# Attention with a compressive memory beside a gated FFN: VectorE's normalization put ahead of an eviction, a product with ones a chain sooner, three operations elsewhere in another order

## The chip, the cores and the metric

The kernel runs on one core of one Trainium2 chip. The metric is device microseconds of one launch. A core has a matrix engine (PE; its weight loads are listed apart as PEld), a vector engine (DVE), an activation engine (ACT), a general engine (POOL) and a queue that issues DMAs (SP). Each works through its own instructions in their order and waits for the others on semaphores.

## The reference, cut to what matters

Two branches read the same x (2048 x 576), and a gate mixes them.

```
for s in range(4):                     # 4 segments of 512, 32 heads of 18
    p = softmax(qs @ ks.T * scale + mask)
    a_dot = p @ vs
    o = g * (phi(qs) @ M) / (phi(qs) @ z) + (1 - g) * a_dot
    M, z = M + phi(ks).T @ vs, z + sum(phi(ks))
a = concat(o) @ wo
b = (gelu(x @ w_gate) * (x @ w_up)) @ w_down      # 576 -> 4608 -> 576
out = sigmoid(x . gate_w) * a + (1 - that) * b
```

## The kernel before, in words

Every large product is made of 16-bit words: a value is split into a high and a low word, and three products (high by high, high by low, low by high) stand for one. Ahead of the split each weight tile is scaled, by a factor from a sum of squares over the whole tile. The FFN products are further made by sums of sub-blocks, with fewer products and more additions.

Projections come first (to about 211 us), then one loop of 72 steps v (`step`, line 1427), then an output stage. PE, ACT, DVE and POOL take their instructions exactly in the order in which the code issues them, so the order written in `step` is the order on each engine. Steps go by fours: `fb = v // 4` is a block of two hidden tiles of the FFN, 18 in all, and `i4 = v % 4` is the place in it. Each step makes gate and up products for two of four column groups of x (into the PSUM banks V, X = tag G, Y = tag U), `gelu` (ACT), the product of the two halves `hidden` (DVE, line 1279, reads the banks G and U), their high and low words (ACT line 1286, POOL line 1294), and eight chains `down` of the block before: six matmuls into one of two buffers of the bank `dn` (line 1256) and an eviction into `acc` on DVE (line 1264, for block 0 line 1262).

Between those lie the attention's pieces. With `k = v - 4`, step v makes the scores of heads 2k and 2k + 1 (line 1171, banks st, dn, pv), adds mask and takes the row maximum on DVE (`piece`, line 1174), makes powers (`powers`: ACT lines 1190 and 1191, POOL line 1192, two transposing DMAs), and multiplies by the values two steps later (`values`, line 1209, bank pv). `normalize(k - 2)` (lines 1219 to 1226) is five DVE instructions which read that bank, divide by the row sums and add into `ob`; after them the bank pv is free.

At `i4 == 1` of every block but the first, `scales(fb + 1, ...)` makes the scale factors for the next block. Its `sums` (line 94) is the product of a matrix of ones with ten sums of squares (`stat`), in f32, which adds over the partitions. ACT has written those sums: `act_squares` at the start of the step, line 89, four activations and four reads of the accumulator. The product goes into the bank pv while the attention runs (fb 1 to 16), so it must wait for the normalization that empties it. Six small DVE instructions follow (lines 268 to 275, on 128 x 2 or 128 x 4 elements). `scales_out` on POOL (lines 281 to 289) ends the work later in the step.

Other places that matter here: `scale_d` (line 394) scales two tiles of the next down weights, in place, on DVE; POOL's `sums_g` (lines 330 to 335) adds weight blocks; `nest_pairs_x` (ACT line 481, DVE line 483) splits sums of x; `result_low` (line 1239) makes the low words of a finished group of four heads, which go to DRAM and are read back, transposed, for the output stage.

The order around the change, at `i4 == 1` (the copy at line 1524 evicts the bank U; X has the tag G, Y has U):

```
product(Y, f, S2, t, 4, 6)
g0 = gl_tile(); dve.tensor_copy(g0, Y)          # L1524
if on(k - 2) and on(k): normalize(k - 2)        # L1219-1226
product(X, f, A12, x1, 2, 6)
rest(X, f, U4, x1, (0,))                        # L1302 into G
some(fb - 1, early[2:3])                        # one chain down
scales(fb + 1, bank("pv") if on(k) else None)   # L94, L268-275
product(Y, f, S1, t, 0, 2)                      # L532 into U
```

Of the kernel before, what the change touches and what calls it, by code (L numbers as in the profile page):

```python
# [26 lines left out]
NF = F // P  # L27
NB = NF // 2
# [15 lines left out]
def kernel(ctx: ExitStack, tc: tile.TileContext, xs, wqk, wv, wo, wgu, wd, beta, out):  # L44
# [8 lines left out]
    def bank(tag, bufs=1, dt=F32):  # L53
        return ps.tile([P, 512 if dt == F32 else 1024], dt, name=tag, tag=tag, bufs=bufs)
# [36 lines left out]
    def sums(st, o=None):  # L91

        o = (spare() if o is None else o)[:, : st.shape[1]]
        pe.matmul(o, ones, st, start=True, stop=True)  # L94
        return o
# [168 lines left out]
    def scales(fb, o=None):  # L264

        o = sums(stat[fb % 2].rearrange("p a b -> p (a b)"), o)
        z = wts.tile([P, 6], F32, name="z", tag="z", bufs=2)
        dve.tensor_reduce(z[:, 4:6], o.rearrange("p (a b) -> p a b", a=2), AX.X, OP.add)  # L268
        dve.tensor_scalar(z[:, 0:4], x2, z[:, 4:5], 1e-30, OP.mult, OP.max)
        v = wts.tile([P, 2, 2], F32, name="v", tag="v", bufs=2)  # L270
        pb = wts.tile([P, 2, 4], F32, name="pb", tag="pb", bufs=3)
        dve.tensor_scalar(v[:, 0].bitcast(I32), z[:, 4:6].bitcast(I32), 1, EXP, OP.logical_shift_right, OP.bitwise_and)
        dve.tensor_scalar(pb[:, 0].bitcast(I32), z[:, 0:4].bitcast(I32), EXP, None, OP.bitwise_and)
        dve.tensor_scalar(v[:, 1].bitcast(I32), v[:, 0].bitcast(I32), EXP, None, OP.bitwise_xor)
        dve.tensor_scalar(pb[:, 1].bitcast(I32), pb[:, 0].bitcast(I32), EXP, None, OP.bitwise_xor)
        scl_a[fb] = v, pb
# [27 lines left out]
    def scale_g(f, cols=slice(0, KT * P)):  # L304
        if f < NF:
            r = raw_g[f].rearrange("p (a b) -> p a b", a=2)[:, :, cols]
            dve.tensor_scalar(r, r, scl[f // 2][0][:, 0:1], None, OP.mult)
# [16 lines left out]
    def sums_g(f):  # L324
        if f >= NF:
            return
        r = raw_g[f]
        g0, g2, u0, u2 = (r[:, o : o + 2 * P] for o in (0, 2 * P, KW, KW + 2 * P))
        g4, u4 = r[:, 4 * P : KW], r[:, KW + 4 * P :]
        pool.tensor_tensor(g2, g0, g2, OP.add)  # L330
        if f < 2 or f % 2 == 0:
            pool.tensor_tensor(g0, u0, g0, OP.subtract)
        pool.tensor_tensor(u0, g2, u0, OP.subtract)
        pool.tensor_tensor(u2, u2, u0, OP.subtract)
        pool.tensor_tensor(g4, u4, g4, OP.subtract)
# [28 lines left out]
    def nest_odd(b):  # L364
        if b < NB:
            nest_w[b] = nest_tile()
            r = raw_g[2 * b + 1]
            pool.tensor_tensor(nest_part(b)[1], r[:, KW : KW + 2 * P], r[:, : 2 * P], OP.subtract)

    def nest_pairs(b, i, what):  # L370
        if b >= NB:
            return
        a, r = nest_part(b)
        src, o = ((a, W00), (r[:, P:], W11), (r, WS3), (a, WS2))[i]
        n = src.shape[1]
        hi, lo = (nest_w[b][:, (o + 7 * j) * P : (o + 7 * j) * P + n] for j in range(2))
        if "h" in what:
            act.activation(hi, src, AF.Copy)
        if "l" in what:
            pool.tensor_tensor(lo, src, hi, OP.subtract)  # L380

    def nest_sums(b):
        if b >= NB:
            return
        a, r = nest_part(b)
        a0, a1, r0, r1 = a[:, :P], a[:, P:], r[:, :P], r[:, P:]
        pool.tensor_tensor(r1, r0, r1, OP.add)
        pool.tensor_tensor(r0, a0, r0, OP.subtract)
        pool.tensor_tensor(a0, r1, a0, OP.subtract)
        pool.tensor_tensor(a1, a1, a0, OP.subtract)  # L390

    def scale_d(f):
        r = raw_d[f]
        dve.tensor_scalar(r, r, scl[f // 2 + 1][0][:, 1:2], None, OP.mult)
# [66 lines left out]
    def nest_x(p):  # L461
        t = flat(kept["xt"][p][:, 8:15])
        return t[:, : 7 * HX], t[:, 7 * HX :]
# [13 lines left out]
    def nest_pairs_x(p, half):  # L477
        r, sc = sums_x[p][1, 2], xsc[:, 2 * p : 2 * p + 1]
        hi, lo = (t[:, 3 * HX :] for t in nest_x(p))
        if half == 0:  # L480
            act.activation(hi, r, AF.Copy, scale=sc)
        else:
            dve.scalar_tensor_tensor(lo, r, sc, hi, OP.mult, OP.subtract)
# [40 lines left out]
    def gl_tile():  # L524
        return mp2.tile([P, L], F32, name="gl", bufs=3)

    def product(o, f, a, x, h, l, start=False):

        w = pair_g[f]
        for k in range(2):  # L530
            for i, b in ((0, h), (0, l), (1, h)):
                pe.matmul(o, w[:, i, (a + k) * P : (a + k + 1) * P], x[:, b + k],  # L532
                          start=start and k == 0 and i == 0 and b == h, stop=k == 1 and i == 1,
                          skip_group_check=True)
# [570 lines left out]
    with tc.tile_pool(name="keep", bufs=2, side="right", reuse_waits="tile") as kp, ExitStack() as tail:  # L1105
# [106 lines left out]
        def normalize(kk):  # L1212
            hf, k = divmod(kk, H)
            b = pvb.pop(kk)
            o = b[:, : 8 * VC].rearrange("p (q c) -> p q c", c=VC)

            sm = b[:, 8 * VC : 8 * (VC + DH)].rearrange("p (q d) -> p q d", d=DH)
            rd = ap_.tile([P, 8], F32, name="ord", bufs=1)
            dve.tensor_reduce(sm, o[:, :, : 2 * DH].rearrange("p q (a d) -> p q d a", a=2), AX.X, OP.add)  # L1219
            dve.reciprocal(rd.unsqueeze(2), o[:, :, 2 * DH :])  # L1220
            for i in range(2):
                b = slice(4 * i, 4 * i + 4)
                dve.scalar_tensor_tensor(sm[:, b], sm[:, b], gha[:, 2 * hf + i, k : k + 1],
                                         rd[:, b].unsqueeze(2).to_broadcast([P, 4, DH]), OP.mult, OP.mult)
            od = obs[kk // 4][:, :, (k % 4) * DH : (k % 4 + 1) * DH]
            dve.tensor_tensor(od, od, sm, OP.add)
# [69 lines left out]
        def gelu(f, c, o, t):  # L1296
            act.activation(t, o, AF.Gelu_apprx_tanh, scale=scl[f // 2][0][:, 2 + c : 3 + c])  # L1297
# [18 lines left out]
                scale_g(n0 + 2)  # L1316

        def weights_nest(fb, i4, at):
            if i4 == 1 and at == 2 and fb:
                for f in (2 * fb, 2 * fb + 1):  # L1320
                    scale_d(f)
            if i4 == 2 and at == 1:
                if fb:
                    scale_g(2 * fb + 3, FRONT)
                    sums_g(2 * fb + 2)
                nest_odd(fb + 1)
            if i4 == 2 and at == "late":
                for i in range(2):
                    nest_pairs(fb + 1, i, "hl")
                nest_sums(fb + 1)  # L1330
            if i4 == 2 and at == 2:
                for i in (2,) if fb else (2, 3):
                    nest_pairs(fb + 1, i, "hl")
            if i4 == 3 and at == 0 and fb:
                nest_pairs(fb + 1, 3, "hl")
# [91 lines left out]
        def step(v):  # L1427

            f, p = divmod(v, 2)
            fb, i4 = divmod(v, 4)  # L1430
            c, e = 2 * p, 2 * p + 1
            k = v - LAG
            on = lambda i: 0 <= i < 2 * H
            early = range(8 * i4, 8 * i4 + 5)
            late = range(8 * i4 + 5, 8 * i4 + 8)
            some = lambda b, js: chains(b, js) if b >= 0 else None
            put = lambda a, i: puts[a](i) if a in puts else None
# [12 lines left out]
            at = (fb + 1, 0) if i4 == 3 and fb + 1 < NB else (fb, 1) if i4 == 0 and fb else None  # L1450
# [9 lines left out]
            one = (2 if fb and i4 < 2 else 1) + (v == 4)  # L1460
# [19 lines left out]
                last_sum(1, 1)  # L1480
            if v == 1:
                nest_sums_x(1)
            if v in (2, 3):
                nest_pairs_x(v - 2, 0)
            if v == 1:
                scale_result()
            if v != 4:
# [29 lines left out]
                product(V, f, A22, x2_, 0, 4)  # L1517
            rest(V, f, G4, x1, (0,) if fb else (0, 1))
            product(Y, f, S2, t, 4, 6)
            g0 = gl_tile()  # L1520
            if fb and i4 >= 2:
                dve.tensor_tensor(g0, Y, g1, OP.add)
# [14 lines left out]
            if v == 0:  # L1537
                scales(fb + 1)
                scales_out(fb + 1)
            if on(k - 2) and on(k):  # L1540
                normalize(k - 2)
            product(X, f, A12, x1, 2, 6)
            rest(X, f, U4, x1, (0,) if fb else (0, 1))
            some(fb - 1, early[max(one, 2):3])
            if fb and i4 == 1:
                scales(fb + 1, bank("pv") if on(k) else None)
            product(Y, f, S1, t, 0, 2)
            rest(Y, f, G4, x2_, (0,) if fb else (0, 1))
            if fb:
                low_rests(f, (V, G4, x1), (Y, G4, x2_))  # L1550
            if on(k):
                puts[2 * k] = scores(2 * k)
            put(2 * k, 1)
            dve.tensor_tensor(g1, Y, g1, OP.add)  # L1554
            gelu(f, e, g1, g1)
            if v == 3:
                nest(at, 0)
            if fb:
# [210 lines left out]
        with tc.manual_schedule(engines=ORDERED):  # L1769
# [17 lines left out]
            fb = NB - 1  # L1787
# [88 lines left out]
```

## Time and profile before

| | |
|---|---|
| time, median of 3 runs | 1574.23 us (1574.0 to 1575.9) |
| the profiled execution | 1574.2 us, of which the span is 1572.5 |
| granted TensorE clock | 1.000 |
| PE busy | 1557.9 us (99%), 12220 matmuls |
| DVE busy | 1266.5 us (81%) |
| ACT busy | 1207.4 us (77%) |
| POOL busy | 1127.8 us (72%) |

The page has the busy time of each engine, the chain of work that ended last, and the costliest groups of instructions. The trace has every instruction with its start and duration, and for each engine's idle time the instruction whose end let it go on. In a row of the timeline the first number is the start in us from the span's start, the second the duration in us; a bracket gives the idle time of the engine ahead of it and what ended that. Matmuls overlap, so a row's duration reaches into the next row; what a group costs is read from start to start.

### The profile page before, as it was taken

Reading aid. Unit: us, or ns where it says so; the run is one execution under the profiler, and the core shown is the slowest. Engines: PE = TensorE matmul, PEld = TensorE weight load, DVE = VectorE, ACT = ScalarE, POOL = GpSimd, SP = SyncE. Lnnn points to the kernel's source line nnn. Section 1 sums busy time; section 2 is a strip of 40 time slices with the busy share of each in tenths; the row PEclk is TensorE's granted clock in tenths of the full one; section 3 lists DMA queues with packets and bytes.
Section 4 is the critical chain, followed back from the end, with each engine's and each line's share of the span. In section 5 each row is a group of like instructions: output and inputs, shape, how many; then the busy total and the mean of one; then the engine's idle time right before and its main releaser. Section 6 shows DMA issues by size and latency. Waiting matters only on the chain.

```text
span 1572.5 us, 33940 instructions
## 1 busy us (share of the span) xinstructions
PE 1557.9 (99%) x12220; PEld 954.0 (61%) x12220; DVE 1266.5 (81%) x3254; ACT 1207.4 (77%) x2059; POOL 1127.8 (72%) x1220
## 2 busy tenths in 40 slices
PE   9999999999999999999999999999999999999999
PEld 5765655565656656555656565666656566656577
DVE  6878976878888888888888878888888888887665
ACT  7567544888888888888888888888888888887421
POOL 4355565878777768686877877787868686787597
PEclk9999999999999999999999999999999999999999
DMA  6533332567858676877767787768677777764546
GB/s 231 213 125 125 130 118 67 116 127 122 147 120 150 119 151 133 126 132 137 143 119 135 124 143 129 143 119 165 133 133 135 136 136 134 134 113 98 125 86 167
DMA packets 472833, 209.97 MB, mean 134 GB/s; under 512 B 427688, under 2 KB 437416, under 8 KB 472152
## 3 DMA queue, kind: packets, MB, share of 16 engines
q1 hardware_dynamic: 472664, 207.80, 64.7%
q8 instruction: 96, 1.57, 0.4%
q14 instruction: 73, 0.60, 0.1%
HBM read 91.87 MB, written 27.26 MB: 76 GB/s over the span
## 4 chain that ended last, share of the span: by engine, by line
PE 87%; DVE 5%; POOL 5%; ACT 1%; issue 1%; DMA 0%; SPq 0%; DVEq 0%; POOLq 0%; ACTq 0%
PE dn L1256 24%; PE U L532 16%; PE G L532 10%; PE V L532 6%; PE V L1376 5%; PE pv L1209 4%; PE st L412 3%; PE dn L419 2%; PE U L1302 2%; PE U L412 1%; PE G L412 1%; PE G L1307 1%; PE st L1171 1%; PE V L1307 1%; POOL pairg L1692 1%; PE V L1302 1%
## 5 line engine op out<-in xcount | busy, mean ns | idle before, releaser
L1192 POOL TENSOR_TENSOR pb<-pb,ph 128x896 f16<-128x896 f32 (+1 forms) x256 | 368.6, 1440 | 260.9 <-ACT ph L1191 250.8
L532 PEld LDWEIGHTS <-pairg 128*128 128x128 f16 x2592 | 248.1, 98 | 258.7 <-issue 12.7
L1256 PE MATMUL dn<-paird,hhr 128*128 128x288 f16 x2115 | 328.9, 286 | 0.9 <-DVE mx L1174 0.9
L1190 ACT ACTIVATE pb<-pb,mb,esc 128x512 f32<-128x512 f32 (+3 forms) x512 | 304.9, 642 | 5.5 <-issue 0.4
L1264 DVE SCALAR_TENSOR_TENSOR acc<-dn,ev,acc 128x288 f32<-128x288 f32 x533 | 262.6, 513 | 39.3 <-PE dn L1256 33.8
L1256 PEld LDWEIGHTS <-hhr 128*128 128x128 f16 x2160 | 207.3, 98 | 80.7 <-issue 13.1
L1256 PE MATMUL dn<-paird,hhd 128*128 128x288 f16 x1275 | 210.0, 286 | 1.2 <-DVE mx L1174 1.2
L532 PE MATMUL G<-x,pairg 128*128 128x512 f16 x864 | 209.9, 379 | 0.9 <-DVE gl L1279 0.8
L532 PE MATMUL U<-xt,pairg 128*128 128x512 f16 x864 | 209.9, 379 | 0.4 <-DVE U L1478 0.4
L1191 ACT ACTIVATE ph<-pb 128x896 f16<-128x896 f32 (+1 forms) x256 | 188.6, 737 | 8.1
L345 POOL TENSOR_TENSOR pairg<-raw,pairg 128x384 f16<-128x384 f32 (+2 forms) x144 | 157.7, 1117 | 17.7 <-ACT pairg L341 17.7
L1174 DVE CUSTOM_DVE_ANT_0 pb<-st,mask 128x512 f32<-128x512 f32 (+1 forms) x256 | 157.1, 614 | 0.7 <-DMA pt<-pb 0.7
L1256 PEld LDWEIGHTS <-hhd 128*128 128x128 f16 x1296 | 124.6, 98 | 53.8 <-issue 8.5
L1174 DVE CUSTOM_DVE_ANT_0 pb<-dn,mask 128x256 f32<-128x256 f32 (+1 forms) x192 | 67.0, 373 | 77.6 <-PE dn L1171 75.9
L1376 PE MATMUL V<-xt,nest 128*128 128x256 f16 x714 | 105.5, 272 | 0.2 <-DVE hold L1392 0.2
L532 PE MATMUL U<-x,pairg 128*128 128x512 f16 x432 | 105.0, 379 | 0.4 <-DVE gl L1554 0.3
L532 PE MATMUL V<-x,pairg 128*128 128x512 f16 x426 | 103.8, 379 | 0.1
L1297 ACT ACTIVATE gl<-gl,sc 128x512 f32<-128x512 f32 x110 | 75.7, 714 | 33.8 <-DVE gl L1554 22.3
L1185 ACT ACTIVATE mb<-mx,esc 128x4 f32<-128x4 f32 x128 | 36.6, 286 | 70.4 <-DVE mx L1174 70.4
L1209 PEld LDWEIGHTS <-pt 128*128 128x128 f16 x2560 | 80.8, 96 | 13.1 <-issue 8.4
L1294 POOL TENSOR_TENSOR hhr<-gl,hhr 128x512 f16<-128x512 f32 x64 | 78.5, 1232 | 10.9 <-ACT hhr L1286 10.8
L1209 PE MATMUL pv<-vt,pt 128*128 128x37 f16 x2560 | 85.0, 179 | 0.0
(369 smaller groups left out, 3123.9 us busy)
## 6 DMA issues: line engine op xcount, KB each, us to landing
raw<-in_wgu_dram SPq DMA_DIRECT2D x36, 640.0 KB
rawd<-in_wd_dram SPq DMA_DIRECT2D x36, 288.0 KB
qt<-qk SPq DMA_DIRECT2D x132, 72.0 KB
kt<-qk SPq DMA_DIRECT2D x132, 72.0 KB
qk<-stage SPq DMA_DIRECT2D x36, 256.0 KB
qt<-qk SPq DMA_DIRECT2D x132, 36.0 KB
kt<-qk SPq DMA_DIRECT2D x132, 36.0 KB
vp<-vstage SPq DMA_DIRECT2D x16, 296.0 KB
```

The costliest lines, as they stand in the source:

```text
L345: pool.tensor_tensor(spot(f, *p, 1), raw_g[f][:, p[0] : p[1]], spot(f, *p, 0), OP.subtract)
L412: pe.matmul(o, w(k, a), x[:, i], start=n == 0, stop=n == 13, skip_group_check=True)
L532: pe.matmul(o, w[:, i, (a + k) * P : (a + k + 1) * P], x[:, b + k], start=start and k == 0 and i == 0 and b == h, stop=k == 1 and i == 1, ...
L1174: dve.tensor_tensor_reduce(scored(a, qi), out[qi], mask[:, L - (qi + 1) * P :], 1.0, -3e38, OP.add, OP.max, mx[a][:, qi : qi + 1])
L1190: act.activation(r, r, AF.Exp, bias=b[:, qi : qi + 1], scale=esc[:, 0, c : c + 1])
L1191: act.activation(h[:, cols], p, AF.Copy)
L1192: pool.tensor_tensor(low[:, cols], p, h[:, cols], OP.subtract)
L1209: pe.matmul(ov, pr[:, 10 * i + COL[qi] // P + kb], v[:, 4 * e + kb, c0 : c0 + VC], start=kb == 0 and i == 0, stop=kb == qi and i == 1)
L1256: pe.matmul(o[:, :NH], hh[:, a, q * P : (q + 1) * P], w[:, b, n * NH : (n + 1) * NH], start=i == 0, stop=i == 5)
L1264: dve.scalar_tensor_tensor(av, o[:, :NH], ev, av, OP.mult, OP.add)
L1294: pool.tensor_tensor(hh[:, 1], t, hh[:, 0], OP.subtract)
L1376: pe.matmul(o, w[:, (7 * c + i) * P : (7 * c + i + 1) * P], x[d], start=start and n == 0, stop=n == 2, skip_group_check=True)
```

## The change

Five edits, all of them in the order of instructions; none is added or taken away.

```
@@ weights_nest
-            if i4 == 1 and at == 2 and fb:
+            if i4 == 1 and at == 2 and 0 < fb < NB - 1:
                 for f in (2 * fb, 2 * fb + 1):
                     scale_d(f)
@@ step
-            if v in (2, 3):
-                nest_pairs_x(v - 2, 0)
+            if v == 2:
+                nest_pairs_x(0, 0)
+            if v == 2 * NF - 2:
+                for n in (2 * fb, 2 * fb + 1):
+                    scale_d(n)
...
             product(Y, f, S2, t, 4, 6)
+            both = on(k - 2) and on(k)
+            if both and i4 == 1:
+                normalize(k - 2)
             g0 = gl_tile()
...
-            if on(k - 2) and on(k):
+            if both and i4 != 1:
                 normalize(k - 2)
             product(X, f, A12, x1, 2, 6)
             rest(X, f, U4, x1, (0,) if fb else (0, 1))
-            some(fb - 1, early[max(one, 2):3])
             if fb and i4 == 1:
                 scales(fb + 1, bank("pv") if on(k) else None)
+            some(fb - 1, early[max(one, 2):3])
...
-            put(2 * k, 1)
+            if v != 4:
+                put(2 * k, 1)
             dve.tensor_tensor(g1, Y, g1, OP.add)
+            if v == 4:
+                put(2 * k, 1)
             gelu(f, e, g1, g1)
+            if v == 3:
+                nest_pairs_x(1, 0)
```

In words: (1) at `i4 == 1`, in the 15 blocks fb 2 to 16, the normalization stands ahead of the copy from U; (2) at `i4 == 1`, in 17 blocks, the scale factors of the next block stand ahead of the third chain `down` instead of behind it; (3) at v = 4 the mask addition of one piece of scores stands behind the addition that empties U; (4) at v = 3 ACT's split of a sum of x stands behind the two gelu; (5) `scale_d` of the last two tiles moves from the end of step 69 into step 70, behind the copy of G into U.

DVE in one of the 15 blocks, around the small instructions of the scale factors (the lines from 1484 on have moved by 3 to 11; L1524 is L1530 now):

```order
-L1524 COPY gl<-U 128x512
-L1219 TENSOR_REDUCE pv<-pv 128x144
-L1220 RECIPROCAL ord<-pv 128x8
-L1223 SCALAR_TENSOR_TENSOR pv<-pv,gha,ord 128x72 x2
-L1226 TENSOR_TENSOR ob<-ob,pv 128x8x18
-L1264 SCALAR_TENSOR_TENSOR acc<-dn,ev,acc 128x288
+L1219 TENSOR_REDUCE pv<-pv 128x144
+L1220 RECIPROCAL ord<-pv 128x8
+L1223 SCALAR_TENSOR_TENSOR pv<-pv,gha,ord 128x72 x2
+L1226 TENSOR_TENSOR ob<-ob,pv 128x8x18
+L1530 COPY gl<-U 128x512
 L268 TENSOR_REDUCE z<-pv 128x2
```

The five instructions of the normalization have changed places with the copy, and the eviction of the chain (L1264), which stood ahead of the six instructions L268 to L275, now stands behind L275.

PE at the same place, the first of the 17 blocks, where the product with ones (L94) now stands:

```order
 L1302 LDWEIGHTS pairg
 L1302 MATMUL G<-x_1132,pairg 128x512
+L94 MATMUL pv<-stat_88,ones 128x10
 L1256 LDWEIGHTS hhr_2747
 L1256 MATMUL dn<-paird,hhr_2747 128x288
```

L94 follows the last matmul into G directly, and the six matmuls of the chain come behind it.

DVE at the end of the loop, steps 69 and 70 (L1279 are the two halves' products, from G and from U; L1239 the low words of a result; L1478 the copy of G into U; L394 `scale_d`):

```order
 L1279 SCALAR_TENSOR_TENSOR gl<-G,sc,gl 128x512
+L1279 SCALAR_TENSOR_TENSOR gl<-U,sc,gl 128x512
+L1239 SCALAR_TENSOR_TENSOR ob<-ob,wsc,oh 128x576
+L1478 COPY U<-G 128x512
 L394 TENSOR_SCALAR rawd<-rawd,sc 128x576 x2
-L1279 SCALAR_TENSOR_TENSOR gl<-U,sc,gl 128x512
-L1239 SCALAR_TENSOR_TENSOR ob<-ob,wsc,oh 128x576
-L1478 COPY U<-G 128x512
```

The two L394 have moved behind three instructions that stood behind them.

## The prediction

> **What bounds the kernel now.** I read the page's first lines, then what PE waited for, then the timeline at each of those waits.
>
> ```profile
> span 1572.5 us, 33940 instructions
> PE 1557.9 (99%) x12220; PEld 954.0 (61%) x12220; DVE 1266.5 (81%) x3254; ACT 1207.4 (77%) x2059; POOL 1127.8 (72%) x1220
> ```
>
> PE sets the time; the others have a fifth or more to spare. So a change of order pays only where PE stands still, and costs only where it makes PE stand. The waits, by releaser (total us, times, longest):
>
> ```profile
> PE pv L94 <- DVE ob L1226: 4.9, 15, 0.3
> PE dn L1256 <- DVE mx L1174: 2.1, 7, 0.3
> ACT mb L1185 <- DVE mx L1174: 70.4, 34, 3.7
> ```
>
> PE's two repeated waits are the first two rows: the product with ones behind the normalization, 15 times, and a chain `down` behind a mask addition, 7 times. The third shows that ACT itself waits, for scores that PE and DVE bring.
>
> The timeline of one of the 15 places, fb = 2:
>
> ```profile
> 354.56 0.69 DVE L1524 COPY gl<-U 128x512 f32<-128x512 f32 x1 [1.63 <-PE U L532]
> 355.17 0.46 DVE L1219 TENSOR_REDUCE pv<-pv 128x144 f32<-128x288 f32 x1
> 355.42 0.19 ACT L89 ACTIVATION_READ_ACCUMULATOR nest<-rawd 128x1 f32 x1
> 355.58 0.38 PE L1302 MATMUL G<-x,pairg 128*128 128x512 f16 x1
> 356.57 0.30 DVE L1226 TENSOR_TENSOR ob<-ob,pv 128x144 f32<-128x144 f32 x1
> 357.02 0.36 PE L94 MATMUL pv<-stat,ones 128*128 128x10 f32 x2 [0.32 <-DVE ob L1226]
> 357.24 1.46 PE L532 MATMUL U<-xt,pairg 128*128 128x512 f16 x6
> 358.35 2.87 POOL L1192 TENSOR_TENSOR pb<-pb,ph 128x896 f16<-128x896 f32 x2 [0.21 <-ACT ph L1191]
> 358.40 1.86 DVE L275 TENSOR_SCALAR pb<-pb 128x4 int32<-128x4 int32 x1
> 359.44 0.54 PE L1256 MATMUL dn<-paird,hhd 128*128 128x288 f16 x3
> 359.81 0.53 PE L1256 MATMUL dn<-paird,hhr 128*128 128x288 f16 x3
> 360.64 0.53 PE L1256 MATMUL dn<-paird,hhd 128*128 128x288 f16 x3 [0.30 <-DVE mx L1174]
> ```
>
> DVE stands idle 1.63 us, copies, and only then normalizes, to 356.87; L94 starts 0.15 later. The second wait has another cause: the small L275 takes 1.86 us beside POOL's L1192, and the mask addition of the bank dn queues behind it.
>
> **Term 1, L94.** The same stretch, from the last matmul into G to the first of the next product into U, at fb = 1, where no normalization is in the way:
>
> ```profile
> 283.07 0.38 PE L1302 MATMUL G<-x,pairg 128*128 128x512 f16 x1
> 283.51 0.19 ACT L89 ACTIVATION_READ_ACCUMULATOR nest<-rawd 128x1 f32 x1
> 284.16 1.46 PE L532 MATMUL U<-xt,pairg 128*128 128x512 f16 x6
> 285.85 0.38 DVE L275 TENSOR_SCALAR pb<-pb 128x4 int32<-128x4 int32 x1
> 286.38 1.89 POOL L1192 TENSOR_TENSOR pb<-pb,ph 128x896 f16<-128x896 f32 x1 [0.17 <-ACT ph L1191]
> ```
>
> It takes 1.09 us there and 357.24 - 355.58 = 1.66 here: a wait costs 0.57, not the 0.32 in the bracket, since the weight loads and the overlap of matmuls are lost too. [...] With the normalization ahead of the copy, its 1.70 us (355.17 to 356.87) fill the idle 1.63; the copy moves by about 0.1 and the bank pv is free near 354.7. PE reaches L94 0.22 after 355.58 (six matmuls of that width take 1.30 from start to start). So the wait goes: 15 x 0.57 = 8.5 us.
>
> What is late next there is L94's other input. ACT's last sum of squares ends at 355.61, 0.03 after the matmul into G starts; with 0.15 for the signal, 0.18, against 0.22: just in time, and nothing is charged. At fb = 1 it ends at 283.70, 0.63 after: L94, a chain sooner, then waits 0.63 + 0.15 - 0.22 = 0.56, where it waited for nothing. I charge 0.6 us, once.
>
> **Term 2, the chain behind the mask addition.** PE's three matmuls take 0.37 (359.44 to 359.81), so the next chain was due at 360.18 and started at 360.64: 0.46 us, 7 times. L275 fell in behind L1192 because it came at 358.40, just after that started. Now L94's sum is there 1.2 us earlier, and the six instructions run beside POOL's L330 to L335. At fb = 1 they already do: L275 ends at 286.23, right behind L335 (286.38 - 0.17 = 286.21, by the bracket) and 0.15 ahead of L1192. Later blocks show the free case:
>
> ```profile
> 946.10 0.17 DVE L275 TENSOR_SCALAR pb<-pb 128x4 int32<-128x4 int32 x1
> ```
>
> So L275 should end near L335's end (358.35 - 0.21 = 358.14), and the eviction L1264 behind it near 358.7. The next chain into that bank comes at 359.44 - 0.57 = 358.87. It holds by 0.05. Gain 7 x 0.46 = 3.2 us.
>
> **Terms 3 to 5, once each.** Steps 3 and 4, then the end of the loop:
>
> ```profile
> 252.96 1.13 ACT L481 ACTIVATE xt<-acc,xsc 128x1024 f16<-128x1024 f32 x1
> 254.00 1.32 ACT L1297 ACTIVATE gl<-gl,sc 128x512 f32<-128x512 f32 x2
> 254.35 0.59 PE L1302 MATMUL U<-x,pairg 128*128 128x512 f16 x2
> 254.73 0.75 DVE L1279 SCALAR_TENSOR_TENSOR gl<-G,sc,gl 128x512 f32<-128x512 f32 x1 [1.67 <-ACT gl L1297]
> 255.54 0.81 PE L532 MATMUL G<-x,pairg 128*128 128x512 f16 x3 [0.59 <-DVE gl L1279]
> 268.02 0.42 DVE L1174 CUSTOM_DVE_ANT_0 pb<-dn,mask 128x256 f32<-128x256 f32 x1 [2.86 <-PE dn L1171]
> 268.29 0.53 PE L1256 MATMUL dn<-paird,hhd 128*128 128x288 f16 x3
> 268.37 0.69 DVE L1554 TENSOR_TENSOR gl<-U,gl 128x512 f32<-128x512 f32 x1
> 269.11 1.24 PE L532 MATMUL U<-x,pairg 128*128 128x512 f16 x5 [0.28 <-DVE gl L1554]
> 1464.74 0.94 DVE L394 TENSOR_SCALAR rawd<-rawd,sc 128x576 f32<-128x576 f32 x2
> 1467.20 0.38 PE L1302 MATMUL V<-x,pairg 128*128 128x512 f16 x1
> 1467.26 0.69 DVE L1478 COPY U<-G 128x512 f32<-128x512 f32 x1
> 1468.00 0.81 PE L532 MATMUL U<-xt,pairg 128*128 128x512 f16 x3 [0.42 <-DVE U L1478]
> ```
>
> Step 3: with L481 behind the gelu, L1297 starts 1.04 sooner and L1279 ends near 254.5. PE's product into G is due at 254.35 + 2 x 0.22 = 254.79 instead of 255.54: 0.75. Step 4: L1554 stands behind the mask addition, and DVE idles 2.86 until PE has made its scores at 268.02; U, which L1554 reads, is complete before PE turns to those scores. So it starts by 268.02 at the latest and somewhat sooner, is done before 268.7, and PE's product into U is due at 268.29 + 0.37 = 268.66 instead of 269.11: 0.45. End: without L394 ahead, the copy is held only by the product into G; PE is due at 1467.42 and I allow it 1467.5 instead of 1468.00: 0.5. L1239's DMAs to the output stage leave sooner too (line 1239 stood behind L394), so POOL's work at the end does not give this back. These three lie between their brackets (0.59 + 0.28 + 0.42 = 1.3) and 0.75 + 0.45 + 0.58 = 1.8; I take 1.7.
>
> **The sum.** 8.5 - 0.6 + 3.2 + 1.7 = 12.8 us. The profiled execution took 1574.2, the median 1574.23, so both give 1561.4 us. A measurement of this kernel can tell about 0.2%, 3.1 us, from no change.
>
> **Rivals.** First, a new small wait in every block. POOL's last instruction of `scales_out` ends before DVE scales the down weights, and the product into G needs what DVE does next:
>
> ```profile
> 952.79 0.22 POOL L289 TENSOR_TENSOR ev<-gate,we 128x16 f32<-128x16 f32 x1
> 953.29 0.94 DVE L394 TENSOR_SCALAR rawd<-rawd,sc 128x576 f32<-128x576 f32 x2
> 954.14 0.75 DVE L1279 SCALAR_TENSOR_TENSOR gl<-G,sc,gl 128x512 f32<-128x512 f32 x1
> 955.14 1.03 PE L532 MATMUL G<-x,pairg 128*128 128x512 f16 x4
> ```
>
> PE and DVE come 0.57 earlier, so L394 at 952.72, against POOL's L289 at 952.79, which follows ACT and stays. If L394 is held behind it as L275 was behind L1192, until 953.01, L1279 comes up to 0.29 late; it has 955.14 - 954.89 - 0.15 = 0.1 to spare. A wait of 0.2 costs 0.2 + 0.2 of lost overlap: 15 x 0.4 = 6.0, and 1567.4. For it speaks the 1.86 of L275; against it, that L394 comes 0.07 ahead of L289 and would go first. [...] Chance 0.2.
>
> Second, slower. L1264 now stands behind L275. If L275 misses the gap between L335 and L1192 (0.21 at fb = 2, 0.17 at fb = 1), it is held to the end of L1192's first half, about 358.35 + 1.88 = 360.2; L1264 is done at 360.7, and the chain due at 358.87 starts near 360.9: 2.0 us, where the same accident cost 0.46 before. In all 15 blocks that is 30 us, 1591.4; in the 7 with this alignment 14, 1575.4. It decides at 8 blocks. Against it: at fb = 1 the gap was smaller and L275 got in. Chance 0.04, half of it slower.
>
> Third, the gain is given back: PE, 1.0 us sooner per block, meets words that ACT or POOL have not made, and only the single terms stay, 1574.2 - 1.7 = 1572.5. Against it stand the 70.4 us, in 34 waits of 2.1 on average, for which ACT alone waits for PE's scores. Chance 0.06. Fourth, the change does only part: term 2 stays because L275 meets another POOL instruction ahead of the mask addition. Then 1564.6. Chance 0.1.
>
> **How the numbers follow.** The forecast has 0.6, the first rival 0.2, the second 0.04, the third 0.06, the fourth 0.1. Faster by over 0.2%: 0.6 + 0.2 + 0.1 = 0.9; same: 0.06 and the half of the second, 0.08; slower 0.02. The range goes from 1559.5 (fb = 1 costs nothing, the single terms their upper value, and a free L94 hides under the wider matmul, some 0.08 each) to the first rival, 1567.5; that leaves out the second and the third, 0.1, and some of the rest.
>
> **What would show it.** Right: no PE row at L94 for L1226, no row at L1256 for L1174, no L275 over 0.5 us, 1.1 us from L1302 to L532 in all blocks, one wait of L94 for L89 at fb = 1, and blocks all some 72.5 us apart. Wrong: PE waiting for L1264 ahead of a chain (second rival), for L1279 ahead of G in each block (first), or L94 waiting for L89 in all 15.

## The result, and the profile after

| | before | after |
|---|---|---|
| time, median of 6 runs each | 1574.12 us (1573.83 to 1575.9) | 1561.07 us (1560.78 to 1561.94) |
| ratio | | 0.9916, 95% interval 0.9903 to 0.9929 |
| the profiled execution, span | 1574.2, 1572.5 us | 1560.9, 1559.2 us |

The forecast was 1561.4 us. The first lines of the page after:

```profile
span 1559.2 us, 33941 instructions
PE 1552.6 (100%) x12220; PEld 954.3 (61%) x12220; DVE 1263.5 (81%) x3254; ACT 1205.7 (77%) x2059; POOL 1132.8 (73%) x1220
```

The span fell by 13.3 us, PE's busy time by 5.3 and its idle time by 8.0 (from 14.6 to 6.6): part of what the waits cost stood in the profile as busy time. DVE's one instruction more, 33941 for 33940, is a semaphore instruction; the operations are the same in number. What PE still waited for after, longest first:

```profile
PE G L813 <- POOL onesb L808: 1.0, 1, 1.0
PE st L412 <- DVE stage L664: 0.4, 1, 0.4
PE pv L94 <- ACT nest L89: 0.3, 1, 0.3
PE dn L704 <- DMA acc<-in_wv_dram: 0.3, 1, 0.3
PE st L412 <- ACT wp L112: 0.2, 1, 0.2
PE G L532 <- DVE gl L1279: 0.2, 1, 0.2
```

Both repeated waits are gone, and nothing that repeats has come in their place. Two rows are new, once each: L94 behind the sums of squares, and L704 behind a DMA. The second lies at 7.02 us, in the projections, far ahead of every edit, and comes and goes between runs: this same kernel, run again below, does not show it. The timeline after, in the block fb = 2 (L1530 is the copy, L1524 before):

```profile
353.45 0.30 DVE L1226 TENSOR_TENSOR ob<-ob,pv 128x144 f32<-128x144 f32 x1
353.76 0.69 DVE L1530 COPY gl<-U 128x512 f32<-128x512 f32 x1
354.62 0.19 ACT L89 ACTIVATION_READ_ACCUMULATOR nest<-rawd 128x1 f32 x1
354.78 0.38 PE L1302 MATMUL G<-x,pairg 128*128 128x512 f16 x1
354.85 0.34 PEld L94 LDWEIGHTS pv<-stat,ones 128*128 128x128 f32 x2 [0.19 <-ACT nest L89]
355.00 0.29 PE L94 MATMUL pv<-stat,ones 128*128 128x10 f32 x2
355.53 0.60 DVE L269 TENSOR_SCALAR z<-x,z 128x4 f32<-128x4 f32 x1
355.87 1.46 PE L532 MATMUL U<-xt,pairg 128*128 128x512 f16 x6
356.18 0.74 POOL L334 TENSOR_TENSOR raw<-raw 128x256 f32<-128x256 f32 x1
356.24 0.70 DVE L274 TENSOR_SCALAR v<-v 128x2 int32<-128x2 int32 x1
356.86 0.16 DVE L275 TENSOR_SCALAR pb<-pb 128x4 int32<-128x4 int32 x1
356.93 0.50 DVE L1264 SCALAR_TENSOR_TENSOR acc<-dn,ev,acc 128x288 f32<-128x288 f32 x1
357.54 2.88 POOL L1192 TENSOR_TENSOR pb<-pb,ph 128x896 f16<-128x896 f32 x2 [0.21 <-ACT ph L1191]
358.07 0.54 PE L1256 MATMUL dn<-paird,hhd 128*128 128x288 f16 x3
```

The normalization ends at 353.75, the copy follows at once, and from the matmul into G to the product into U it is 355.87 - 354.78 = 1.09 us, where it was 1.66. The weight load of L94 waits 0.19 for ACT, hidden under the wide matmul ahead of it: L94 itself has no bracket. L275 takes 0.16 and ends 0.52 ahead of L1192; the eviction L1264 ends at 357.43, 0.64 ahead of the chain at 358.07.

At fb = 1 the product with ones does wait, and the stretch is 283.35 - 281.70 = 1.65 us, 0.56 longer than before:

```profile
281.70 0.38 PE L1302 MATMUL G<-x,pairg 128*128 128x512 f16 x1
282.13 0.19 ACT L89 ACTIVATION_READ_ACCUMULATOR nest<-rawd 128x1 f32 x1
282.38 0.39 PE L94 MATMUL pv<-stat,ones 128*128 128x10 f32 x2 [0.29 <-ACT nest L89]
283.35 0.38 PE L532 MATMUL U<-xt,pairg 128*128 128x512 f16 x1
```

The place of the first rival, in the step behind (364.49 and on are the next step's products):

```profile
363.65 0.27 POOL L287 TENSOR_SCALAR we<-pb,v 128x4 f32<-128x4 f32 x1
363.94 0.94 DVE L394 TENSOR_SCALAR rawd<-rawd,sc 128x576 f32<-128x576 f32 x2
364.00 0.52 POOL L289 TENSOR_TENSOR ev<-gate,we 128x16 f32<-128x16 f32 x1
364.80 0.75 DVE L1279 SCALAR_TENSOR_TENSOR gl<-G,sc,gl 128x512 f32<-128x512 f32 x1
365.80 0.59 PE L532 MATMUL G<-x,pairg 128*128 128x512 f16 x2
```

L394 comes 0.06 ahead of L289 and runs its usual 0.94; here it is POOL that is held, 0.52 instead of 0.22. The product into G has no bracket.

### The profile page after: what moved, and what is told of

Read it like the earlier page. It is cut to its first block, busy times and chain, and to the rows that moved or that the text cites. A ratio compares the mean times of both kernels' runs of the same rounds, so it can differ in the third digit from the quotient of the medians.

```text
span 1559.2 us, 33941 instructions
## 1 busy us (share of the span) xinstructions
PE 1552.6 (100%) x12220; PEld 954.3 (61%) x12220; DVE 1263.5 (81%) x3254; ACT 1205.7 (77%) x2059; POOL 1132.8 (73%) x1220
## 5 line engine op out<-in xcount | busy, mean ns | idle before, releaser
L1192 POOL TENSOR_TENSOR pb<-pb,ph 128x896 f16<-128x896 f32 (+1 forms) x256 | 368.6, 1440 | 244.5 <-ACT ph L1191 234.5
L1264 DVE SCALAR_TENSOR_TENSOR acc<-dn,ev,acc 128x288 f32<-128x288 f32 x533 | 262.5, 513 | 38.4 <-PE dn L1256 32.9
L1256 PEld LDWEIGHTS <-hhr 128*128 128x128 f16 x2160 | 207.3, 98 | 77.5 <-issue 11.5
L1174 DVE CUSTOM_DVE_ANT_0 pb<-st,mask 128x512 f32<-128x512 f32 (+1 forms) x256 | 157.1, 614 | 0.4 <-DMA pt<-pb 0.4
L1174 DVE CUSTOM_DVE_ANT_0 pb<-dn,mask 128x256 f32<-128x256 f32 (+1 forms) x192 | 67.1, 374 | 78.2 <-PE dn L1171 76.5
L341 ACT ACTIVATE pairg<-raw 128x384 f16<-128x384 f32 (+2 forms) x144 | 77.8, 587 | 8.5 <-DVE raw L307 6.1
```

What stands on the lines that cost most here:

```text
L341: act.activation(spot(f, *p, 0), raw_g[f][:, p[0] : p[1]], AF.Copy)
L1174: dve.tensor_tensor_reduce(scored(a, qi), out[qi], mask[:, L - (qi + 1) * P :], 1.0, -3e38, OP.add, OP.max, mx[a][:, qi : qi + 1])
L1192: pool.tensor_tensor(low[:, cols], p, h[:, cols], OP.subtract)
L1256: pe.matmul(o[:, :NH], hh[:, a, q * P : (q + 1) * P], w[:, b, n * NH : (n + 1) * NH], start=i == 0, stop=i == 5)
L1264: dve.scalar_tensor_tensor(av, o[:, :NH], ev, av, OP.mult, OP.add)
```

## The experiments

The kernels ran on three chips, with the kernel before beside each. Its median was 1574.52 with the first four below, 1574.8 with two more (the old order at fb = 1, and L268 twelve times over) and 1572.75 with the last three (without the sooner product, the change itself, and L268 eight times over). The kernels before and after of the section above form a group of their own. Unless said otherwise, times are compared within a group.

**The normalization alone** (the kernel before with edit 1).

```
+            both = on(k - 2) and on(k)
+            if both and i4 == 1:
+                normalize(k - 2)
             g0 = gl_tile()
...
-            if on(k - 2) and on(k):
+            if both and i4 != 1:
                 normalize(k - 2)
```

> Only the normalization moves ahead of the copy; the product with ones stays behind the chain. Theory (terms 1 and 2 are separate, and term 2 needs the product with ones sooner): the 15 waits of L94 go, 8.5 us, but L275 still comes at about 2.7 us after the matmul into G, where POOL's L1192 starts at 2.76, so most of the 7 waits behind L1174 stay: 1565 to 1566 us. Rival (the normalization brings all, the product with ones a chain sooner brings nothing but the wait at fb = 1): 8.5 + 3.2, 1562.4 us, and no row of PE for L1174.

Measured 1562.98 us, ratio 0.9927 (0.9911 to 0.9944): the rival's number. No row of PE for L1226 or for L1174 is left, and the blocks are 72.51 us apart (L94 at 356.38 and 428.89 in this kernel, 357.02 and 430.55 before). The timeline at fb = 2, with the matmul into G, L94 and L275:

```profile
355.43 0.38 PE L1302 MATMUL G<-x,pairg 128*128 128x512 f16 x1
356.38 0.29 PE L94 MATMUL pv<-stat,ones 128*128 128x10 f32 x2
358.03 0.17 DVE L275 TENSOR_SCALAR pb<-pb 128x4 int32<-128x4 int32 x1
358.20 1.89 POOL L1192 TENSOR_TENSOR pb<-pb,ph 128x896 f16<-128x896 f32 x1 [0.23 <-ACT ph L1191]
```

L275 starts 0.17 ahead of L1192 and slips through. My theory, that both edits were needed for term 2, fell: with L94 unhindered, L275 starts 2.60 us after the matmul into G instead of 2.82, and L1192 at 2.77.

**The product with ones alone** (the kernel before with edit 2).

```
-            some(fb - 1, early[max(one, 2):3])
             if fb and i4 == 1:
                 scales(fb + 1, bank("pv") if on(k) else None)
+            some(fb - 1, early[max(one, 2):3])
```

> Only the product with ones moves ahead of the chain; the normalization stays behind the copy. Theory: L94 now waits for the normalization with no chain to cover it, until 1.44 us after the matmul into G instead of 0.22, so the stretch from L1302 to L532 takes about 2.5 us instead of 1.66 in 15 blocks (12 us more), the eviction L1264 stands behind a late L275 in 7 blocks (another 0.4 each), and fb = 1 costs 0.6: 1588 us, within 3. Rival (a wait costs only its bracket, 1.2 against 0.32): the same sign and 13 us, so only the stretch itself tells. Rival that the chain sooner is good by itself: below 1574 us.

Measured 1587.17 us, ratio 1.008 (1.0065 to 1.0095). At fb = 2:

```profile
356.18 0.38 PE L1302 MATMUL G<-x,pairg 128*128 128x512 f16 x1
357.62 0.36 PE L94 MATMUL pv<-stat,ones 128*128 128x10 f32 x2 [1.06 <-DVE ob L1226]
358.57 1.46 PE L532 MATMUL U<-xt,pairg 128*128 128x512 f16 x6
358.98 1.87 DVE L275 TENSOR_SCALAR pb<-pb 128x4 int32<-128x4 int32 x1
360.77 0.51 DVE L1264 SCALAR_TENSOR_TENSOR acc<-dn,ev,acc 128x288 f32<-128x288 f32 x1
361.33 0.53 PE L1256 MATMUL dn<-paird,hhd 128*128 128x288 f16 x3 [0.49 <-DVE acc L1264]
```

The stretch takes 2.39 us, 1.30 over the free 1.09 with a bracket of 1.06: again about 0.25 beyond the bracket. In 7 blocks L275 is held by L1192, the eviction now stands behind it, and the chain waits 0.5 us for L1264. (The table of waits has 8 places and 4.0 us; the eighth, 0.60, lies in step 58.) So the second rival's mechanism is real here; it cost little because PE was late as well. Without edit 1, edit 2 does harm.

**The three single moves alone** (edits 3 to 5).

> Only the three single moves at steps 3, 4 and at the loop's end. Theory: 0.75 + 0.45 + 0.5, 1572.4 us. Rival (work behind them takes it back): 1574.1 us, with the shift between the two traces gone by the loop's end.

Measured 1571.95 us, ratio 0.9984 (0.9975 to 0.9993), 2.6 us below before, 2.1 by the profiled spans (1570.4 against 1572.5 for the trace of before, from another group). The shift between these two traces is still 2.1 us at the last step. So they add, and nothing takes them back. Of the excess over 1.7, some 0.35 us arises in step 59, where PE waited 0.20 for a DVE copy (L1392) before and not here.

**The two block edits together, without the single moves** (edits 1 and 2).

> The normalization and the product with ones together, none of the three single moves. Theory (the terms add): 1561.1 + 1.8, 1562.9 us, with the three waits of PE at the single places back. Rival (what the single moves bring is taken back in the blocks): 1561.1 us.

Measured 1563.58 us (1563.07 to 1564.28), ratio 0.993 (0.9916 to 0.9945): nearer to the theory than to its rival. With the normalization alone it was 1562.98 (1562.58 to 1563.51); these times overlap, but the traces show what the sooner product does, a stretch of 1.65 us instead of 1.09 at fb = 1, and no gain in the seven blocks of term 2, 72.5 us apart either way. PE's waits at the three single places and at L1392 are back.

**The change with the old order at fb = 1.**

```
+            if i4 == 1 and fb == 1:
+                some(fb - 1, early[max(one, 2):3])
             if fb and i4 == 1:
                 scales(fb + 1, bank("pv") if on(k) else None)
-            some(fb - 1, early[max(one, 2):3])
+            if i4 != 1 or fb != 1:
+                some(fb - 1, early[max(one, 2):3])
```

> The change, but in the first block (fb = 1) the product with ones stays behind the chain. Theory: the one wait of L94 for the sums of squares goes, L1302 to L532 takes 1.1 us there instead of 1.65, and nothing else changes: 0.56 us less than the change, 1560.5 us, which the time can hardly tell and the timeline can. Rival (the stretch at fb = 1 is taken back a step later, by DVE or ACT): the change's time, 1561.1 us, with the shift gone by the next block.

Measured 1560.3 us (1560.03 to 1562.06, 5 runs), ratio 0.9912 (0.9898 to 0.9926). The span is 1558.5 against 1559.2, the row of L94 for L89 is gone, and the stretch at fb = 1 is 1.09 us. The time itself, from another group than the change's, cannot tell the two apart.

**The normalization and the single moves, without the sooner product**, beside the change itself on the same chip.

> The change without the product with ones a chain sooner: the normalization ahead of the copy and the three single moves. Revised theory (the normalization alone frees L275, the sooner product brings nothing and costs the wait at fb = 1): 0.56 us less than the change, 1560.4 us, L275 ends at 2.70 to 2.77 us after the matmul into G, level with the start of L1192, and is still not held. Rival (with the single moves L1192 and L275 shift against each other and the 7 waits come back): 3.2 us more, 1563.7 us.

> The change again, to stand beside the variant without the sooner product on one chip: 1561.1 us, 0.6 above that variant by the revised theory, 2.6 below it by the rival.

Measured 1561.83 us (1561.01 to 1562.16) without, ratio 0.9929 (0.9916 to 0.9943), and 1562.31 us (1561.92 to 1562.87) with, ratio 0.9934 (0.9921 to 0.9946). The difference of 0.5 us has the sign and size of the wait at fb = 1, but the intervals overlap. L275 is not held by L1192 in any block. At fb = 2 it comes at:

```profile
357.23 0.17 DVE L275 TENSOR_SCALAR pb<-pb 128x4 int32<-128x4 int32 x1
357.43 1.89 POOL L1192 TENSOR_TENSOR pb<-pb,ph 128x896 f16<-128x896 f32 x1 [0.26 <-ACT ph L1191]
```

What the sooner product does is widen that 0.20 us to 0.72 (357.21 to 357.93 in the change beside it). It buys room, not time.

**The small instructions late, on purpose** (the change, with L268 issued twelve times over; it writes the same numbers each time).

```
-        dve.tensor_reduce(z[:, 4:6], o.rearrange("p (a b) -> p a b", a=2), AX.X, OP.add)
+        for _ in range(12 if 2 <= fb < NB else 1):
+            dve.tensor_reduce(z[:, 4:6], o.rearrange("p (a b) -> p a b", a=2), AX.X, OP.add)
```

> The change, with the first of the six small instructions (L268) issued twelve times over in 16 blocks, so that L275 comes some 1.5 us later and meets POOL's L1192: the accident of the second rival, made on purpose. Second rival's price: L275 held to the end of L1192's first half, 4.6 us after the matmul into G, the eviction L1264 done at 5.2, the chain due at 3.29 starts near 5.35: 2.0 to 2.2 us a block, 16 blocks, 1593 to 1596 us; if L275 is held by the second half too, a further 1 us a block, 1612 us. If the price was wrong and the accident costs 0.46 us a block as before: 1568 us.

Measured 1632.38 us, ratio 1.0378 (1.0358 to 1.0397). One of the six is held by L1192's first half, another by its second, and the chain waits 2.85 us for the eviction (lines are one higher):

```profile
362.06 2.88 POOL L1193 TENSOR_TENSOR pb<-pb,ph 128x896 f16<-128x896 f32 x2 [0.22 <-ACT ph L1192]
362.26 1.70 DVE L270 TENSOR_SCALAR z<-x,z 128x4 f32<-128x4 f32 x1
364.07 0.88 DVE L275 TENSOR_SCALAR v<-v 128x2 int32<-128x2 int32 x1
364.94 0.51 DVE L1265 SCALAR_TENSOR_TENSOR acc<-dn,ev,acc 128x288 f32<-128x288 f32 x1
365.50 0.53 PE L1257 MATMUL dn<-paird,hhd 128*128 128x288 f16 x3 [2.85 <-DVE acc L1265]
```

That is my dearer case, 1612, and still 20 us short. The waits for the eviction, by the table of waits:

```profile
PE dn L1257 <- DVE acc L1265: 43.0, 16, 2.9
PE dn L1257 <- DVE acc L1263: 2.8, 1, 2.8
```

These 45.8 us are not all of the 79.1 between the profiled spans of this kernel and the change (1638.3, the longest of the four executions, and 1559.2 from another group). The mean granted clock of this execution was 0.977, where all kernels above show 1.000, so PE also ran slower: by an estimate 0.023 of 1638.3 us, 37.7, some of which passed while PE stood still. The two together cover the difference, and the price of 1612 had no term for the clock.

**The same, eight times over.**

> As the run with the first small instruction twelve times over, but eight times, so that L275 or the one before it is held by L1192's first half alone: the second rival's price by itself. Second rival: the chain due at 3.29 us after the matmul into G starts near 5.4, 2.1 us a block, 16 blocks, and if the clock stays at 1.00 nothing more: 1595 us. If a gap of 2.1 us also lowers the granted clock, up to 1.4 us a block more, 1617 us. If L275 slips in ahead of L1192: 1562 us.

Measured 1570.88 us, ratio 0.9985 (0.9975 to 0.9995), against 1562.31 for the change beside it: neither 1595, for being held in every block, nor 1562, for slipping by. In the profiled execution L275 (here L276) starts within 0.05 us of L1192 (L1193) in the first 8 blocks, is held in three of them and slips by in five; in the later blocks it ends just ahead. Where it is held, at fb = 2:

```profile
359.49 1.88 POOL L1193 TENSOR_TENSOR pb<-pb,ph 128x896 f16<-128x896 f32 x1 [0.26 <-ACT ph L1192]
359.50 1.90 DVE L276 TENSOR_SCALAR pb<-pb 128x4 int32<-128x4 int32 x1
361.32 0.51 DVE L1265 SCALAR_TENSOR_TENSOR acc<-dn,ev,acc 128x288 f32<-128x288 f32 x1
361.88 0.80 PE L1257 MATMUL dn<-paird,hhd 128*128 128x288 f16 x3 [1.84 <-DVE acc L1265]
```

So one accident costs PE a bracket of 1.84 us where I had 2.0 for the whole; but from this block's L94 to the next (356.90 to 433.00, 76.1 us against the usual 72.6) 3.5 us were lost, and the clock was lower there:

```profile
360.00:363.00 3.00, 1.16 (x8) 0.81 (x7) 3.00 (x6) 2.95 (x5) 2.92 (x3) 0.83 0.56 120
363.00:366.00 3.00, 3.00 (x13) 1.61 (x12) 2.12 (x7) 2.10 (x4) 2.58 (x8) 0.60 1.30 137
366.00:369.00 3.00, 3.00 (x32) 2.18 (x30) 1.45 (x5) 0.49 (x2) 0.15 (x1) 1.00 1.00 285
```

The columns are the stretch, its length, the busy time of PE, PEld, DVE, ACT and POOL, the granted clock, the DMA share and GB/s. The clock is a mean over each stretch. At 0.83 and 0.60 the first two lose 0.17 and 0.40 of their 3.00 us, 1.7 us together, and with the 1.84 of the wait that makes the 3.5. PE's own pace says the same: three matmuls of a chain take 0.72 us (362.47 to 363.19) where they take 0.36 at fb = 1 (287.85 to 288.21), half the speed. Of the other two places, the one with L276 at 799.53 lost 3.5 us in the same way, and the one at fb = 1 lost 1.85 at a clock of 1.00. Together the three make 8.8 of the 9.9 us between the profiled spans of this kernel and of the change beside it (1570.5 and 1560.6).

## Why the prediction was right

The sum was 12.8 us; the profiled spans differ by 13.3 and the medians by 13.05.

- Term 1, L94: 15 stretches of 1.09 us instead of 1.66, as forecast, 8.5 us. The copy starts 1.02 us ahead of the matmul into G both before and after, so not even the 0.1 allowed for it was lost. That a wait costs more than its bracket held three times: 0.57 for 0.32 before, 1.30 for 1.06 with the product alone, and 0.56 for 0.29 at fb = 1. That the extra 0.25 is lost weight loads and overlap, as the prediction has it, was not tested by itself.
- The charge of 0.6 us at fb = 1: 0.56. In the other 15 blocks ACT came just in time, as worked out (0.18 against 0.22): a bracket on the weight load, none on L94.
- Term 2: the seven blocks lost their 0.46, so they are 1.02 us shorter in all and 72.5 us apart. The size was right, two steps in it were not, so that here the right number is in part luck. The prediction had L275 come out behind L335 and the eviction hold "by 0.05" (its own 358.87 - 358.7 is 0.17, and 0.02 after the 0.15 for the signal). L275 came out ahead of L335, and the eviction held by 0.64: the small instructions up to L273 started before POOL's L334, and L274 took the hold, 0.70 us, to the end of L334. And it counted L94's sum coming 1.2 us earlier as the cause; the normalization alone, with the sum 0.49 us earlier after the matmul into G (0.95 instead of 1.44), did it as well.
- Terms 3 to 5: the shift between the traces grows by 0.76, 0.46 and 0.58 us there, for 0.75, 0.45 and 0.5.
- Not in the sum: 0.35 us at step 59, the wait for L1392. All kernels without the single moves show it there, and none with them does (the one with L268 eight times over has two such waits, in steps 16 and 68). Why it goes was not tried. With it the terms make 13.3 us. Some tenths in single blocks, both ways, remain.

The first rival's place was right and its outcome the other: DVE went first, and L289 was held. The second rival's mechanism exists, shown by the product alone and by the late instructions; the change stays clear of it by half a microsecond. The third (the gain taken back) is refuted by the blocks' distance and by the single moves, which were still whole at the end. Of the fourth a trace was seen, L274 held by L334 for 0.70 us in 16 blocks, with no wait of PE behind it.

What the forecast did not ask is which edit earns what. The normalization alone brings 11.5 us (1574.52 to 1562.98), the single moves 2.6, and the sooner product loses the 0.56 us at fb = 1, by the traces.

## What to carry to other kernels

On an engine that is busy 99% of the time, read each of its remaining waits as a place: compare the stretch with the same stretch where the wait is absent, since the bracket here told 0.3 of 0.57 us. When one engine idles for an operand while work for another engine's next step lies behind it in the queue, put that work into the idle time: five instructions here fitted 1.70 us into a gap of 1.63. And test bundled edits one by one: one of two that looked like a pair earned everything, and the other only widened a margin.

## What the runs showed of the hardware that was not expected

In the profiled execution with L268 eight times over, the clock fell behind two waits of PE, of 1.84 and 1.82 us, and not behind one of 1.78. Behind the first, which ends at 361.88, the clock is 0.83 from 360 to 363 us and 0.60 from 363 to 366; behind the second, which ends at 801.90, it is 0.89 from 800 to 803 and 0.55 from 803 to 806; in the 3 us after both it is 1.00 again. Behind the third, which ends at 287.48 (fb = 1), it is 1.00 from 285 to 297. PE's pace agrees. The same work follows all three, twelve matmuls of chains and six into U: 4.43 and 4.44 us behind the first two (361.88 to 366.31, 801.90 to 806.34), 2.76 behind the third (287.48 to 290.24). From L94 to the next L94 it is 76.1 us with the first and the second and 74.45 with the third, against the usual 72.6: such a wait cost 3.5 us where the clock fell and 1.85 where it did not. In length the three differ by 0.06 us at most; what else decided is not shown.

Two other runs stand on either side. With L268 twelve times over, the waits for the eviction come to 45.8 us, the longest 2.9, and the mean clock of its four executions was 0.977 to 0.983. With the product with ones alone, 15 waits of up to 1.1 us for the normalization left the clock at 1.000.

Which of DVE's small instructions and POOL's went first turned on hundredths of a microsecond. In the first eight blocks with L268 eight times over, L275 and L1192 start within 0.05 us of each other. In three blocks L275 starts 0.01 to 0.05 us behind L1192 (285.15 for 285.10, 359.50 for 359.49, 799.53 for 799.52), takes 1.86 to 1.90, and costs PE 1.8 us of waiting and, in two of them, what the clock took behind it. In the other five it starts in the same hundredth or 0.01 ahead (581.19 for 581.20) and takes 0.17.
